# Whole loads of the moving operands at the changes of half, shared weight tiles and background key folds in a gated attention and MLP kernel

## The chip, the cores and the metric

The kernel runs on one core of a Trainium2 chip. The metric is the device time of one execution in microseconds. Five engines run side by side, each through its own queue in order: PE (TensorE) multiplies, and PEld is its loading of stationary tiles; DVE (VectorE) and ACT (ScalarE) do elementwise work; POOL (GpSimd) and SP (SyncE) here mostly issue DMAs. DMAs carry data between the large memory and the on-chip memory of 128 partitions.

## The reference

S = 2048 tokens, D = 1024, 32 heads of 32, DF = 3584. All in fp32.

```python
g = sigmoid((x * gate_w).sum(-1, keepdims=True))
a = A_ref(x, wqkv, w_phi, wo)
b = (gelu(x @ w_gate) * (x @ w_up)) @ w_down
return g * a + (1 - g) * b

def A_ref(x, wqkv, w_phi, wo):            # per head
    q, k, v = split(x @ wqkv)
    phi_q = concat([softmax(q @ w_phi), softmax(-(q @ w_phi))])
    phi_k = concat([softmax(k @ w_phi), softmax(-(k @ w_phi))])
    kv, z = phi_k.T @ v, phi_k.sum(tokens)
    o = (phi_q @ kv) / (phi_q @ z + 1e-6)
    return heads(o) @ wo
```

## The kernel before

**Split operands.** Every fp32 operand of a matmul is split into a high part in the short format fp32r, which ACT writes (`high`, L56), and a low part, the rest, which DVE subtracts (`low`, L59). A product is three passes, high·high, high·low and low·high (`PASSES`).

**Seven products for eight.** The large products of x are made on 2×2 blocks with seven block products in place of eight, from sums of blocks. The seven stationary operands of a unit come in four tiles: `wgu` for x (2 in turn), `tyz` for y and z (3 in turn), and `v`. The seven moving operands are the blocks x10, x11, x01 and the sums s1 to s4, each of four pieces of 128×512 (256 KB), split into high and low. `w_phi` is folded into the key and query weights by small matmuls (the folds: 16 key folds at L297, 16 query folds later), so that keys and queries come out already multiplied by it.

**Units and halves.** 80 units run one after another in `unit`. Half 0 has the eight value units `v`: the moving side is the value weights, the stationary side blocks of x. Half 1 has the eight key units `k`: the moving side is the folded key weights (`wk_fold`, and its sums `ks`), the stationary side again blocks of x. Half 2 and half 3 take one half of the tokens each as moving side (`in_xT` and its sums `xs`), with q, gate and up weights as stationary side: 4 query units and 14 pairs of gate and up. A unit has seven steps (slots) of one block product, 12 matmuls at L665: 0 a<-x, 1 p<-y, 2 c<-z of the unit before, 3 a<-z, 4 a<-v of the unit before, 5 c11<-x, 6 b<-y. Steps 0 and 3 start new sums in PSUM; ACT copies results on (`c<-b` L696, `c<-a` L709, `b<-a` L711), and DVE subtracts p from them (`less`, L678). Between steps stand fillers: query folds, features (L881) and attention (L1085).

**What sets the order.** A planner written in the kernel records everything in one order. `run_slot` takes, after each step, work from streams (generators that yield earliest slot, latest slot, DVE cost and ACT cost), as a clock of its own lets it fit; an engine's queue then holds its work in that order. SP's loads and POOL's stores are issued where the streams come to them.

**Turns.** Where the half changes (units 8, 16 and 48) all seven moving operands must be replaced while units go on. `change_half` has an order of parts with the step from which the old part is free and the step at which the new one is needed. There are three homes of 256 KB; a piece is loaded into a home (L480) once the piece that was there has been split by ACT and DVE.

**Weights.** `weights` makes the stationary operands of a unit: loads, sums on DVE (L133 to L141), splits. Units of half 2 store them, in part as sums (`tq..`, `tg..`), and half 3 loads them again (y and z: 1 MB each, L518).

**Start.** Unit 0 is done plainly while the value weights come in. Its raw pieces then give the sums s1 to s4 (`w_steps`, L146). Of the 16 key folds, 4 pieces at a time have homes; the others wait for a home and are put between the steps of units 1 and 2. `key_sums` then reads all of `wk_fold` back (4 MB), forms the sums and stores them as `ks`. `gates` forms g in the background.

**Values out.** `split_values` (L160 to L162) splits value results on ACT and DVE and stores them to `vt`, through three homes in turn.

**After the units** the down projection and `wo` run as one product at L1343, 3024 matmuls.

Of the kernel before, what the change touches and what calls it, by code (L numbers as in the profile page):

```python
# [16 lines left out]
P = 128  # L17
# [16 lines left out]
def tile_gated_mix(ctx: ExitStack, tc: tile.TileContext, x, xT, wkT, wqT, wv, w_phi, wo,  # L34
# [45 lines left out]
    def new_quarter(b, k):  # L80
        return ring.tile([P, 2, KC // 2, BLK], F32R, name=f"x{b % 2}{k}", bufs=1)
# [73 lines left out]
    def split_values(m, odd, j, i, dst, src):  # L155

        b, c, g = m // 4 * 2 + 1 - odd, m % 4, 4 * j + 2 * i
        d = dst.rearrange("p (n s d) -> p n s d", s=2, d=64)
        x = src[:, 256 * i:256 * i + 256].rearrange("p (n d) -> p n d", d=64)
        nc.scalar.activation(d[:, :, 0], x, AF.Copy)  # L160
        nc.vector.tensor_tensor(d[:, :, 1], x, d[:, :, 0].bitcast(F32), OP.subtract)
        nc.gpsimd.dma_start(tokens["v"][b][g:g + 2, :, c].rearrange("g p f -> p g f"),  # L162
                            dst.bitcast(F32).rearrange("p (g f) -> p g f", g=2))
# [16 lines left out]
    with tc.manual_schedule(engines={PE, DVE, ACT, SP}):  # L180
# [10 lines left out]
        xb, xs = {}, [None] * 4  # L191
# [26 lines left out]
        for b, k in ((1, 0), (1, 1), (0, 1)):  # L218
            xb[b, k] = new_quarter(b, k)
        x00 = [new_work(k, F32R).rearrange("p (a k) t -> p a k t", a=2) for k in range(2)]  # L220

        def x_plain(blk, kc):
            if (blk, kc // 4) == (0, 0):
                return x00[kc // 2][:, :, kc % 2]
            return xb[blk, kc // 4][:, :, kc % 4]
# [16 lines left out]
        def sum_steps(n):  # L242
            while n and ready:
                i = ready[0]
                if next(x_sums[i], "over") == "over":
                    ready.pop(0)
                    continue
                n -= 1

        bps = []  # L250
        for s in range(KC):
# [5 lines left out]
            high(xq[1][:, 0], src[1])  # L257
            if s == 0:
                nc.vector.tensor_copy(xq[0][:, 0], src[0])
            else:  # L260
                high(xq[0][:, 0], src[0])
            for blk in (1, 0):
                low(xq[blk][:, 1], src[blk], xq[blk][:, 0])
# [12 lines left out]
            for n, (a, e) in enumerate(PASSES):  # L276
                for blk in (1, 0):
                    for f in range(2):
                        nc.tensor.matmul(plain_banks[blk, f], wide_w[a][:, kc, f * P:(f + 1) * P], xq[blk][:, e],
                                         start=s == 0 and n == 0, stop=s == KC - 1 and n == 2)  # L280

        rooms = [stage().rearrange("p (a b) -> p a b", a=2)]
        first_o = stage((0, 1024, block("v", 3)))
        rooms.append(xa.tile([P, 2, BLK], F32, tag="v", name="fold", bufs=1))
        homes = [t[:, n] for t in rooms for n in range(2)]
        homes.append(fa.tile([P, BLK], F32, tag="o2", name="fold", bufs=1))
        order = [(h, kc) for h in range(2) for kc in range(KC)]

        def fold_load(i):
            h, kc = order[i]  # L290
            nc.sync.dma_start(homes[i], wkT[h, kc])

        def fold_piece(i):
            h, kc = order[i]
# [6 lines left out]
            if i in (2, 3, 4):  # L301
                fold_load(i + 3)
            elif 8 <= i < 12:
                fold_load(i + 4)

        for i in range(5):
            fold_load(i)
        split_0, raw_0 = new_work(0), new_work(1)
        homes += homes[2:] + [raw_0[:, n] for n in range(4)] * 2

        x1 = new_weight()
        y1 = xa.tile([P, 2, KC, P], F32R, tag="pts", name="first", bufs=1)
        xs = [(xa if k < 2 else fa).tile([P, 2, KC // 2, BLK], F32R, name=f"s{k + 1}", bufs=1) for k in range(4)]
        SUM_AT = (3, 0, 2, 1)

        def sum_parts(k, kc):
            src, dst = raws[kc][SUM_AT[k]], xs[k][:, :, kc]
            return (lambda: high(dst[:, 0], src)), (lambda: low(dst[:, 1], src, dst[:, 0]))
# [4 lines left out]
        def plain_store(n, j, f):  # L323
            for i in range(2):
                room = split_0[:, 2 * (n % 2) + i] if 2 * n + i < 7 else fp.tile([P, BLK], F32, tag="qx", name="vh", bufs=1)
                split_values(0, 1 - f, j, i, room.bitcast(F32R), raw_0[:, n])
# [19 lines left out]

        first_sums("y")
        sum_steps(100)
# [19 lines left out]
        def run_slot(t, matmuls=12, vector=0.0, scalar=0.0):  # L368
# [6 lines left out]
            while True:  # L375
                best = None
                for s in streams:
                    lo, hi, d, a = (*s[0], 0.0, 0.0)[:4]
                    d *= 0.91
# [38 lines left out]
        def key_sums(pa):  # L418
            for kc in range(KC // 2):
                rs = wide if kc % 2 else [pa[:, 0], pa[:, 1]]  # L420
                for r, j in zip(rs, (1, 0)):
                    nc.sync.dma_start(r.rearrange("p (a b) -> p a b", a=2), wk_fold[j][kc::4].rearrange("k p n -> p k n"))
                if kc % 2 == 0:
                    continue
                yield now[0] + 3, NEVER, 0.0
                for k in (kc - 1, kc):
                    r1, r2 = wide if k % 2 else [pa[:, 0], pa[:, 1]]
                    four = a11, a12, a21, a22 = r1[:, :BLK], r1[:, BLK:], r2[:, :BLK], r2[:, BLK:]
                    for i, _ in enumerate(w_steps(*four)):
                        if i % 2 == 0:  # L430
                            yield now[0], NEVER, 1.4
                    for i, t in enumerate((a22, a11, a21, a12)):
                        nc.gpsimd.dma_start(k_sum[i][:, k, :], t)
                yield now[0] + 1, NEVER, 0.0

        def gates(pa):
            rows = [pa[:, 1], wide[1]]
# [947 lines left out]
```

## Time and profile before

| | |
|---|---|
| median of 3 runs | 2459.62 us (2453.88 to 2465.41) |
| profiled execution | 2455.46 us |
| its span, first to last instruction | 2453.7 us |
| TensorE busy | 2367.0 us |
| mean granted TensorE clock | 0.980 |
| DMA | 657.49 MB, mean 268 GB/s |

Units start at 29.01 (unit 1), 74.24 (2), 97.81 (3), 209.79 (8, first turn), 279.97 (10), 407.07 (16, second turn), 463.73 (18), 1050.85 (47), 1073.57 (48, third turn), 1196.71 (53); the down projection follows from 1763.33. In a timeline row stand start, length (of a group: from its first start to its last end), engine, line, operation and tiles, and in brackets the idle time of that engine before it with what ended it. `x12` at the end counts the instructions in a group.

### The profile page before, as it was taken

The numbers are of one execution on the slowest core, as the hardware profiler recorded it, in microseconds if no ns is written. First come the engines' busy times: TensorE is split into PE (matmuls) and PEld (weight loads), VectorE is DVE, ScalarE is ACT, GpSimd is POOL, SyncE is SP. The second block draws the span as 40 slices with busy tenths as digits, with TensorE's granted clock in tenths as the row PEclk, the third lists the DMA queues.
The fourth block names the chain that finished last, engine by engine and source line by source line (L and its number), as shares of the span: only waits on it lengthen the run. The fifth ranks groups of instructions, "written<-read, shape, count | busy, mean of one in ns | idle before, by whom it ended". The sixth has DMA issues, their size and how long they took to land. (4 is left out here: it accounts for less than half of the span.)

```text
span 2453.7 us, 29604 instructions
## 1 busy us (share of the span) xinstructions
PE 2367.0 (96%) x10414; PEld 1939.4 (79%) x10414; DVE 1755.6 (72%) x2402; ACT 1212.1 (49%) x1702; POOL 393.7 (16%) x625
## 2 busy tenths in 40 slices
PE   7998999899999999988999999999999999999999
PEld 6875787678888888876788877878888888888887
DVE  7565556588887888754688888887375677876874
ACT  5434444555655565543578777776254223322221
POOL 2332332122222222211111111111000000000000
PEclk9998899999999999999999999999999999999999
DMA  6786787788888999989778877777686667887774
GB/s 210 269 297 229 258 280 282 266 297 304 306 294 301 304 296 311 313 308 328 235 258 248 261 253 238 252 234 255 228 307 234 222 232 251 303 296 281 266 276 137
DMA packets 244773, 657.49 MB, mean 268 GB/s; under 512 B 31360, under 2 KB 70288, under 8 KB 228240
## 3 DMA queue, kind: packets, MB, share of 16 engines
q1 hardware_dynamic: 184864, 436.53, 53.0%
q0 software_dynamic: 59488, 218.94, 25.7%
q8 instruction: 82, 1.34, 0.2%
q14 instruction: 67, 0.55, 0.1%
q10 hardware_dynamic: 272, 0.13, 0.0%
HBM read 436.86 MB, written 218.90 MB: 267 GB/s over the span
## 5 line engine op out<-in xcount | busy, mean ns | idle before, releaser
L1343 PE MATMUL po<-tw,wgu 128*128 128x512 f32 x1344 | 309.8, 389 | 0.0
L56 ACT ACTIVATE wgu<-stage 128x1024 fp32r<-128x1024 f32 (+2 forms) x168 | 174.6, 1039 | 250.1 <-DVE stage L1233 160.5
L1343 PEld LDWEIGHTS po<-tw,wgu 128*128 128x128 f32 x1344 | 252.3, 188 | 52.4
L665 PE MATMUL a<-s,tyz 128*128 128x512 f32 x948 | 243.1, 405 | 21.5 <-DMA tyz<-tq0z 5.9
L665 PE MATMUL c<-x,tyz 128*128 128x512 f32 x948 | 236.1, 398 | 18.0 <-ACT c L696 11.0
L665 PE MATMUL a<-x,wgu 128*128 128x512 f32 x948 | 234.9, 398 | 8.5 <-DVE wgu L59 6.7
L665 PE MATMUL b<-s,tyz 128*128 128x512 f32 x936 | 233.0, 398 | 9.2 <-ACT s L56 5.5
L665 PE MATMUL c<-x,wgu 128*128 128x512 f32 x948 | 235.1, 395 | 4.1 <-DVE x L59 2.4
L665 PEld LDWEIGHTS a<-s,tyz 128*128 128x128 f32 x948 | 182.8, 195 | 69.5 <-issue 14.9
L665 PE MATMUL p<-s,tyz 128*128 128x512 f32 x936 | 229.6, 394 | 5.4 <-ACT w L683 5.0
L665 PE MATMUL a<-s,v 128*128 128x512 f32 x948 | 230.8, 392 | 1.6 <-ACT s L56 1.1
L665 PEld LDWEIGHTS c<-x,tyz 128*128 128x128 f32 x948 | 180.7, 192 | 59.7 <-ACT c L696 13.1
L59 DVE TENSOR_TENSOR wgu<-stage,wgu 128x1024 fp32r<-128x1024 f32 (+2 forms) x136 | 162.9, 1197 | 88.5 <-ACT wgu L56 87.3
L665 PEld LDWEIGHTS a<-x,wgu 128*128 128x128 f32 x948 | 181.8, 193 | 48.0 <-DVE wgu L59 7.1
L665 PEld LDWEIGHTS b<-s,tyz 128*128 128x128 f32 x936 | 177.9, 191 | 51.7 <-ACT s L56 8.3
L665 PEld LDWEIGHTS p<-s,tyz 128*128 128x128 f32 x936 | 176.9, 190 | 45.8 <-ACT w L683 6.6
L665 PEld LDWEIGHTS c<-x,wgu 128*128 128x128 f32 x948 | 177.3, 190 | 44.1 <-DVE x L59 4.6
L665 PEld LDWEIGHTS a<-s,v 128*128 128x128 f32 x948 | 178.4, 189 | 40.6 <-ACT s L56 2.0
L1343 PE MATMUL po<-tw,wl 128*128 128x512 f32 x672 | 156.9, 389 | 0.0
L1343 PE MATMUL po<-tyz,wgu 128*128 128x512 f32 x672 | 155.6, 389 | 0.4 <-DVE wgu L59 0.4
L1343 PEld LDWEIGHTS po<-tyz,wgu 128*128 128x128 f32 x672 | 126.0, 188 | 27.0 <-DVE wgu L59 0.8
L1343 PEld LDWEIGHTS po<-tw,wl 128*128 128x128 f32 x672 | 126.0, 188 | 26.3 <-DVE wl L59 0.2
(331 smaller groups left out, 3600.3 us busy)
## 6 DMA issues: line engine op xcount, KB each, us to landing
stage<-lm SPq DMA_DIRECT2D x98, 512.0 KB, 4.5
sr<-in_w_down SPq DMA_DIRECT2D x84, 512.0 KB, 4.9
sl<-lm SPq DMA_DIRECT2D x70, 512.0 KB, 4.8
lm<-h POOLq DMA_DIRECT2D x112, 256.0 KB, 5.7
stage<-in_w_gate SPq DMA_DIRECT2D x42, 512.0 KB, 6.4
stage<-in_w_up SPq DMA_DIRECT2D x42, 512.0 KB, 5.2
vs<-vt SPq DMA_DIRECT2D x32, 512.0 KB, 4.3
zs<-w POOLq DMA_DIRECT2D x32, 512.0 KB, 6.3
```

The lines of the kernel that those rows point to most:

```text
L56: nc.scalar.activation(dst, src, AF.Copy)
L59: nc.vector.tensor_tensor(dst, src, dst_h.bitcast(F32), OP.subtract)
L665: nc.tensor.matmul(dst, w[:, h, 4 * part + kc, :], xq[:, e, kc, :], start=first and kc == 0 and i == 0, stop=kc == 3 and i == 2, skip_grou ...
L1343: nc.tensor.matmul(ps[c], lefts[s][:, a, m, c * P:(c + 1) * P], made[k][:, e, m], start=d == 0 and m == 0 and n == 0, stop=d == n_duo - 1 ...
```

## The change

1. **Moving operands as whole halves.** Each of the seven operands now has a tile for its high and one for its low parts (`x_part`). `change_half` loads all four pieces of an operand at one point (L509), into a home that a table `PLANS` names: the rings of `wgu` ("x") or `tyz` ("y"), the work tiles, or the low tile of another operand that isn't written yet (a number). `change_parts` and `low_part` split them.
2. **Shared weights.** `shares(n)`: units 7 and 8 (value and key block 7) and units 47 and 48 (query block 3 in both halves) use the same stationary tiles. The order of the key units and of the queries in half 3 is changed to that end; the sums of that query block are neither stored nor loaded.
3. **Key folds.** Four folds stand before unit 1; the other twelve are fillers in units 2 to 5 (`key_folds`), with their sums formed from the tiles at hand. Only one group of four pieces is read back. `gates` starts after the first turn.
4. **Copy and subtraction.** At step 0, `move` puts ACT's copy c<-b ahead of DVE's subtraction in halves 0 to 2 (`swap`).
5. **Values out.** Both halves are split together, over four homes.
6. **y and z in half 3** are loaded in two parts of 512 KB (L596).
7. **Start.** The first weight's split and the folds stand ahead of the sums; in unit 1 the steps 1 and 5 are exchanged.
8. The planner counts 0.95 of a DVE cost in place of 0.91. The accumulators of the down projection get other names; its work is the same.

**First place: DVE before unit 1.** The row `wgu<-stage,wgu` of 128×1024 is the low half of the first weight, `raw` and `h` at L146 (now L149) the sums s1 to s4, `first` is y. Before:

```order
L59 TENSOR_TENSOR first_546<-stage_534,first_546 128x1024 [waits Activation_49]
L146 TENSOR_TENSOR raw_342<-raw_342 128x512
L146 TENSOR_TENSOR raw_342<-raw_342 128x512 [waits DVE_49]
L146 TENSOR_TENSOR raw_343<-raw_343 128x512
L146 TENSOR_TENSOR raw_343<-raw_343 128x512 [waits DVE_49] x3
L146 TENSOR_TENSOR raw_347<-h_346,raw_347 128x512
L146 TENSOR_TENSOR h_346<-h_346,h_344 128x512 [waits DVE_49]
L146 TENSOR_TENSOR h_344<-h_344,raw_347 128x512 [waits DVE_49]
L146 TENSOR_TENSOR h_345<-h_345,h_344 128x512 [waits DVE_49]
L59 TENSOR_TENSOR wgu_545<-stage_381,wgu_545 128x1024 [waits Activation_49]
```

Now:

```order
L59 TENSOR_TENSOR wgu_546<-stage_384,wgu_546 128x1024 [waits DMAHW1_49,Activation_49]
L136 TENSOR_TENSOR stage_537<-stage_537 128x512 [waits DMAHW2_49]
L137 TENSOR_TENSOR stage_537<-stage_384,stage_537 128x512 [waits DVE_49]
L59 TENSOR_TENSOR first_547<-stage_537,first_547 128x1024 [waits Activation_49]
L149 TENSOR_TENSOR raw_347<-h_346,raw_347 128x512
L59 TENSOR_TENSOR s1l_549<-raw_341,s1h_548 128x512 [waits Activation_49]
L59 TENSOR_TENSOR s1l_549<-raw_342,s1h_548 128x512 [waits Activation_49]
L59 TENSOR_TENSOR s1l_549<-raw_343,s1h_548 128x512 [waits Activation_49]
L59 TENSOR_TENSOR s1l_549<-raw_347,s1h_548 128x512 [waits Activation_49]
L149 TENSOR_TENSOR raw_342<-raw_342 128x512
L149 TENSOR_TENSOR raw_343<-raw_343 128x512
L149 TENSOR_TENSOR h_346<-h_346,h_344 128x512
```

The first weight's low half has moved from behind ten sums to ahead of them; the remaining sums are spread between later low halves.

**Second place: SP at the third turn**, around unit 48. L480 and L509 are pieces of moving operands, L64 and L534 (L612) a unit's raw and x weights, L518 (L596) y and z. Before:

```order
L480 DMA w0_543<-xs00_152 128x512 x2
L587 DMA o2_8037<-wq7_190 128x512
L480 DMA w0_543<-xs01_153 128x512 x4
L64 DMA stage_8083<-wq2_185 128x1024
L534 DMA wgu_8085<-tq1x_309 128x1024
L480 DMA w0_543<-in_xT 128x512
L518 DMA tyz_8108<-tq0z_307 128x2048
L480 DMA w0_543<-in_xT 128x512 x3
L600 DMA o2_8150<-wq1_184 128x512
L480 DMA w0_543<-xs02_154 128x512 x2
```

Now:

```order
L509 DMA wx_7946<-in_xT 128x512 x4
L509 DMA wy_7970<-xs00_152 128x512 x4
L509 DMA wx_7946<-xs01_153 128x512 x4
L509 DMA s2l_8041<-in_xT 128x512 x4
L669 DMA o2_8046<-wq7_190 128x512
L918 DMA vs_2849<-vt1_149 128x1024
L509 DMA wy_7970<-xs02_154 128x512 x4
L64 DMA stage_8109<-wq0_183 128x1024
L612 DMA wgu_8111<-tq0x_305 128x1024
L509 DMA w0_544<-in_xT 128x512 x3
```

The pieces of an operand, which stood singly among other loads, stand four together, into tiles of several names in place of w0 alone.

**Third place: ACT and DVE at step 0 of a unit in half 2**, here the one in whose turn h_5759 is written. `c_87<-b_86` is the copy, `h_5759<-b_86,w0` the subtraction; the names after "waits" are the semaphores of the engine or DMA queue. ACT before:

```order
L683 ACTIVATE w0_543<-p_5604 128x512 [waits DVE_49]
L56 ACTIVATE v_5752<-o2_5703 128x512 [waits DMAHW6_49,DMASW6_49]
L696 ACTIVATE c_87<-b_86 128x512 [waits DVE_49]
L56 ACTIVATE tyz_5778<-stage_5598 128x1024 [waits DMASW5_49,PE_49]
L858 ACT_TABLE_LOAD
```

ACT now:

```order
L769 ACTIVATE w0_544<-p_5603 128x512 [waits DVE_49]
L56 ACTIVATE v_5749<-o2_5702 128x512 [waits DMAHW7_49,DMASW3_49]
L783 ACTIVATE c_87<-b_86 128x512 [waits PE_49,Activation_49]
L56 ACTIVATE tyz_5777<-stage_5598 128x1024 [waits DMASW2_49]
L948 ACT_TABLE_LOAD [waits DMASW5_49]
```

DVE before:

```order
L678 TENSOR_TENSOR h_5759<-b_86,w0_543 128x512 [waits DMASW4_49,PE_49,Activation_49]
L634 TENSOR_TENSOR h_5759<-h_5759,w0_543 128x512 [waits DVE_49]
L59 TENSOR_TENSOR v_5752<-o2_5703,v_5752 128x512 [waits DMAHW6_49,DMASW6_49,Activation_49]
L59 TENSOR_TENSOR tyz_5778<-stage_5598,tyz_5778 128x1024 [waits DMASW5_49,Activation_49]
L861 TENSOR_REDUCE st_5782<-w1_565 128x32 [waits Activation_49]
```

DVE now:

```order
L764 TENSOR_TENSOR h_5759<-b_86,w0_544 128x512 [waits DMASW1_49,Activation_49]
L716 TENSOR_TENSOR h_5759<-h_5759,w0_544 128x512 [waits DVE_49]
L59 TENSOR_TENSOR v_5749<-o2_5702,v_5749 128x512 [waits DMAHW7_49,DMASW3_49]
L59 TENSOR_TENSOR tyz_5777<-stage_5598,tyz_5777 128x1024 [waits DMASW2_49,PE_49,Activation_49]
L951 TENSOR_REDUCE st_5781<-w1_599 128x32 [waits Activation_49]
```

The places in the queues are the same; only the direction of the wait has turned: ACT waited for DVE, and now DVE waits for ACT.

The core of the diff:

```diff
+    X_NAMES = ("x10", "s1", "s2", "x11", "s3", "s4", "x01")
+    def x_part(i, part, dtype=F32R):
+        pool = ring if i % 3 == 0 else xa if i < 3 else fa
+        return pool.tile([P, KC // 2, BLK], dtype, name=X_NAMES[i] + "hl"[part], bufs=1)
...
         def change_half(t, half):
...
-            homes = [gated(1, 0), *((e2[:, 0], e2[:, 1]) if half == 1 else (gated(0, 0), gated(0, 1)))]
...
+            homes = {}
+            for i, at, home in PLANS[half]:
+                yield t + at, t + at, 0.0
+                while home in busy:
+                    yield now[0] + 1, now[0] + 1, 0.0
...
+                busy[home] = True
+                for j in range(len(x)):
+                    nc.sync.dma_start(x[j], srcs[i][:, j])
+                start(change_parts(half, i, home, x, t, need, srcs[i]))
+        LAST, NEED, busy = (-7, -6, -4, -2, -1, 4, 2), (0, 1, 3, 5, 6, 11, 9), {}
+        SPARE = ((0, -7, "x"), (1, -6, "y"), (2, -4, "x"), (3, -3, 2), (4, -1, "y"))
+        PLANS = {1: (*SPARE, (6, 0, "x"), (5, 3, "y")), 3: (*SPARE, (6, 0, "g"), (5, 3, "z")),
+                 2: ((0, -11, "x"), (2, -5, 1), (1, -5, "x"), (3, -1, "x"), (4, 0, 3), (5, 3, 6), (6, 4, "x"))}
...
+        def shares(n):
+            return n in TURNS and units[n][2] == units[n - 1][2] and units[n][1] + units[n - 1][1] in ("kv", "qq")
...
-                load_parts("z", z)
+                load_part("z", z, 0)
+                yield t + 1, t + 1, 0.0
+                load_part("z", z, 1)
...
-        def move(c, b):
-            subs.append(subs.pop()())
+        def move(c, b, swap=False):
+            if not swap:
+                subs.append(subs.pop()())
             nc.scalar.activation(c, b, AF.Copy)
+            if swap:
+                subs.append(subs.pop()())
...
-                    move(c, b)
+                    move(c, b, before[0] < 3)
...
+            if n and shares(n):
+                right_ops[n] = right_ops[n - 1]
...
+        def key_folds(i, groups):
...
+            for kc in groups:
+                for (h, c), t in zip(pieces, four):
+                    nc.sync.dma_start(t, wkT[h, c] if kc else wk_fold[h][c])
...
+                    fillers.append((0, products, 4, range(1, 7)))
```

In a plan a row is the operand's number, the step from the turn at which its load is issued, and its home.

More of the change, by code (lines that the diff above doesn't have):

```diff
@@ L497, in tile_gated_mix, with low_part @@
+        def low_part(dst, x, h, need, home, j):
+            yield now[0], need - 2, 0.69
+            low(dst, x, h)
+            if j == KC // 2 - 1:
+                del busy[home]
+                if home == "z":
+                    for k in held_homes:
+                        held[k] = False
         HALF = {2: 1, 3: 0}
-        units = [(0, "v", m) for m in range(8)] + [(1, "k", m) for m in (4, 5, 6, 7, 0, 1, 2, 3)]
+        units = [(0, "v", m) for m in range(8)] + [(1, "k", m) for m in (7, 4, 5, 6, 0, 1, 2, 3)]
@@ L511, in weights @@
             seen.add((kind, m))
+            if n + 1 < len(units) and shares(n + 1):
+                again = {}
+            chunk = kind == "k" or kind == "v" and shares(n + 1)
             def keep_parts(i, t):
@@ L557, in weights @@
                     mine["y"] = y
[L558 removed]
+                    if chunk:
                         store_chunk(m, 2, 0, o)
```

295 lines of the change are left out of this document (167 added, 128 removed).

## The prediction

> **What bounds the kernel now.** I read the page's busy table first, then the table of stretches, cut where the kernel turns from one half to the next.
>
> ```profile
> span 2453.7 us, 29604 instructions
> PE 2367.0 (96%) x10414; PEld 1939.4 (79%) x10414; DVE 1755.6 (72%) x2402; ACT 1212.1 (49%) x1702; POOL 393.7 (16%) x625
> 27.31:97.81 70.50, 54.30 (x273) 46.12 (x272) 41.09 (x65) 36.32 (x70) 21.20 (x33) 0.88 0.61 207
> 97.81:209.79 111.98, 102.81 (x421) 80.59 (x419) 72.34 (x118) 43.81 (x81) 37.21 (x55) 0.95 0.81 277
> 209.79:279.97 70.18, 58.32 (x192) 40.17 (x193) 36.34 (x56) 30.17 (x54) 17.25 (x24) 0.81 0.70 230
> 407.07:463.73 56.66, 46.54 (x170) 32.37 (x168) 28.36 (x40) 25.22 (x39) 7.71 (x13) 0.94 0.77 277
> 463.73:1050.85 587.12, 584.11 (x2669) 485.57 (x2668) 476.43 (x624) 340.12 (x451) 143.87 (x235) 1.00 0.89 301
> 1050.85:1196.71 145.86, 126.17 (x525) 101.08 (x524) 70.71 (x105) 55.95 (x92) 24.35 (x41) 0.94 0.86 303
> ```
>
> The columns are the stretch, its length, the busy time of PE, PEld, DVE, ACT and POOL, then granted clock, DMA share and GB/s. TensorE is busy for 96% of the span, and the change takes no matmul away: what can be won is what TensorE waits, and the clock that it loses around its waits. The stretches are the start (units 1 and 2), the value units 3 to 7, turn 1 (units 8, 9), turn 2 (16, 17), the body of half 2 (18 to 46) and turn 3 (47 to 52).
>
> Next comes the price of an undisturbed step, from the timeline of TensorE (start, length, group):
>
> ```profile
> 91.47 1.05 PE L297 MATMUL misc<-bp,w 128*128 128x128 f32 x8
> 92.28 2.98 PE L665 MATMUL c<-x,wgu 128*128 128x512 f32 x12
> 397.94 1.11 PE L881 MATMUL misc<-pts,vs 128*128 128x256 f32 x8
> 398.89 2.91 PE L665 MATMUL a<-s,v 128*128 128x512 f32 x12
> 1146.66 2.88 PE L665 MATMUL c<-x,wgu 128*128 128x512 f32 x12
> 1149.38 2.88 PE L665 MATMUL b<-s,tyz 128*128 128x512 f32 x12
> ```
>
> From start to start a product step (12 matmuls) costs 2.72 us, a fold 0.81, a feature filler 0.95. A unit has 7 steps, so the loss of a stretch is its length less these:
> - start: 70.50 − 12 steps (32.64) − 16 folds (12.96) = **24.9**
> - values: 111.98 − 35 steps (95.2) = **16.8**
> - turn 1: 70.18 − 14 steps (38.08) − 3 fillers (2.4) = **29.7**
> - turn 2: 56.66 − 14 steps (38.08) = **18.6**
> - half 2: 587.12 − 203 steps (552.2) − 232 filler matmuls (29 groups of 8 at 0.95, 27.6) = **7.3**
> - turn 3: 145.86 − 42 steps (114.24) − 3 fillers (2.8) = **28.8**
>
> Together 126 us. TensorE's waits proper are length less busy (11.9 in turn 1, 10.1 in turn 2, 19.7 in turn 3); the rest is slow clock (0.81 granted in turn 1).
>
> ```profile
> 1069.12 4.61 PE L665 MATMUL b<-s,tyz 128*128 128x512 f32 x12 [1.79 <-ACT b L711]
> 1141.12 2.98 PE L665 MATMUL a<-s,tyz 128*128 128x512 f32 x12 [1.50 <-DMA tyz<-tq2z]
> ```
>
> The bracket is the idle time before. After 1.79 us the next step took 4.61 instead of 2.88, after 1.50 only 2.98: a wait of about 1.8 us or more costs 1.7 us again in slow clock. The Trainium skill, "TensorE: Matmul & The Clock Gate", section "HAM oscillation — how this bites in real kernels", puts the limit at "no PE-idle gaps >~3.4µs"; this trace pays at 1.79 already, and the measurement decides. By that rule removing turn 1's short gaps would give back the gaps alone; that is a rival below.
>
> **The change part by part.**
>
> *Start, 24.9.*
>
> ```profile
> 28.23 4.20 DVE L146 TENSOR_TENSOR raw<-raw 128x512 f32<-128x512 f32 x6
> 35.13 1.22 DVE L59 TENSOR_TENSOR wgu<-stage,wgu 128x1024 fp32r<-128x1024 f32 x1
> 36.40 3.90 PE L665 MATMUL a<-x,wgu 128*128 128x512 f32 x10 [6.68 <-DVE wgu L59]
> 50.12 2.05 PE L297 MATMUL misc<-bp,fold 128*128 128x128 f32 x8 [4.38 <-DMA fold<-in_wkT]
> ```
>
> The first weight's low half stood behind the sums on DVE; it now stands ahead of them, so the 6.68 goes, and its slow step. Folds that waited for reloads (4.38 here) become fillers taken when their data are there; their 16 × 0.81 us on TensorE stay. But the sums (each 0.70, six in the row of 4.20) now stand ahead of later operands: step 3 of unit 1 waits for z behind six of them and two of its own sums (8 × 0.70 = 5.6), and step 1 of unit 2 for a low half that stands behind a value store. I keep 20 of the 24.9: **−5**. Bounds: +5, if both waits come at full length with a slow step, to −13 (both gaps above with 1.7 each, no new wait).
>
> *Values, 16.8.*
>
> ```profile
> 189.39 4.77 PE L665 MATMUL p<-s,tyz 128*128 128x512 f32 x12 [2.30 <-ACT w L683]
> 215.71 0.38 ACT L160 ACTIVATE w<-c 128x256 fp32r<-128x256 f32 x1 [4.38 <-DMA vt<-w]
> ```
>
> ACT's split waits for the store that last used its home, and the copy of p stands behind it: such a stall costs TensorE 2.30 + 1.89. A fourth home gives each store one more split of time; ACT's wait is still there at times, but shorter than what TensorE has in hand. Against this twelve folds with their loads (3 MB) and sums run here. I keep about two stalls of 4.2: **−8**, bounds −13 (one) and +4 (five, if fold fillers wait for their data).
>
> *Turns 1 and 2, 29.7 and 18.6.*
>
> ```profile
> 228.91 0.63 ACT L56 ACTIVATE s<-w 128x512 fp32r<-128x512 f32 x1 [3.26 <-DMA w<-ks]
> 233.30 0.63 ACT L56 ACTIVATE x<-w 128x512 fp32r<-128x512 f32 x1 [3.77 <-DMA w<-wk]
> 421.84 0.63 ACT L56 ACTIVATE x<-w 128x512 fp32r<-128x512 f32 x1 [3.72 <-DMA w<-in_xT]
> 2100.00:2160.00 60.00, 60.00 (x266) 49.71 (x265) 50.30 (x50) 18.35 (x18) 3.79 (x7) 1.00 0.94 340
> ```
>
> Each of 28 pieces is loaded only when one of three homes has been converted: the latency of a 256 KB load stands in the chain again and again, with DMA only 0.70 busy. The new plan asks for four pieces at once, most parts two to five steps (5 to 14 us) ahead of need, so a latency is paid once a part and mostly beside matmuls. Converting a part is 4 × 0.63 on ACT and 4 × 0.69 on DVE, about 2.8 us, one step. Turn 1 also loses unit 8's weights, 1.25 MB of loads and their splits. What is left is the rate: turn 1 moved 70.18 × 230 = 16.1 MB, less 1.25 is 14.9; at 340 GB/s, the rate in the last row, 43.8 us against 40.5 without loss. Turn 2's 56.66 × 277 = 15.7 MB take 46.2 against 38.1, part of it loaded earlier. I leave 6.7 in each, about 1.6 stalls of 4.2: **−23** and **−12**. Bounds: one half of the loss kept (−15, −9), or two thirds of a stall left (−27, −16).
>
> *Turn 3, 28.8.*
>
> ```profile
> 1077.76 0.42 SPq L518 DMA_DIRECT2D tyz<-tq0z x1
> tyz<-tq0z SPq DMA_DIRECT2D x1, 1024.0 KB, 9.9
> 1087.81 5.46 PE L665 MATMUL a<-s,tyz 128*128 128x512 f32 x12 [5.88 <-DMA tyz<-tq0z]
> 1117.56 4.74 PE L665 MATMUL a<-s,tyz 128*128 128x512 f32 x12 [2.82 <-DMA tyz<-tq1z]
> stage<-in_w_gate SPq DMA_DIRECT2D x42, 512.0 KB, 6.4
> ```
>
> The z operand, 1 MB, is asked for at the unit's start and needed 3 steps (8.2 us) later, and takes 9.9. Unit 48 now shares unit 47's weights: 3.5 MB of loads and 2.75 MB of stores go, and with them the 5.88 and its slow step (2.58). The later z loads come in halves; step 3 needs the first alone, and 512 KB takes 6.4 by the last row, so 2.82, 1.50 and two more of its kind shrink to little. Part loads go ahead as in turn 2. The stretch moved 145.86 × 303 = 44.2 MB; 38 MB take 112 us at 340 GB/s, under the 117 without loss. I leave two stalls, 8.8: **−20**; bounds −10 (the parts' 1 MB loads take the place of z) and −26.
>
> *Half 2 and the swap, 7.3.*
>
> ```profile
> 708.87 0.69 DVE L678 TENSOR_TENSOR w<-b,w 128x512 f32<-128x512 f32 x1 [1.96 <-PE b L665]
> 712.40 0.58 ACT L696 ACTIVATE c<-b 128x512 f32<-128x512 f32 x1
> 712.53 1.22 DVE L861 TENSOR_REDUCE st<-w 128x32 f32<-128x1024 f32 x1 [1.77 <-ACT w L858]
> 715.91 1.23 DVE L59 TENSOR_TENSOR tyz<-stage,tyz 128x1024 fp32r<-128x1024 f32 x1 [1.77 <-ACT tyz L56]
> 716.76 2.99 PE L665 MATMUL a<-s,tyz 128*128 128x512 f32 x12
> ```
>
> ACT's copy of b now goes first and DVE's subtraction waits for it: a wait is added on DVE. Behind it stand the low half of v, the reduction and the low half of z, which TensorE takes at 716.76. If the copy still ends at 712.98, then 0.69 + 0.69 + 1.22 + about 0.35 bring DVE to 715.93 for the z half, which began at 715.91: no loss, but no cover either. The copy itself can go earlier, since it no longer waits for DVE. **−1** for the half with the k units; bounds −4 and +10 (a third of 29 units late by 1 us).
>
> *Half 3.*
>
> ```profile
> 1224.81 0.69 DVE L678 TENSOR_TENSOR h<-b,w 128x512 f32<-128x512 f32 x1 [3.71 <-DMA la<-h]
> 1226.17 4.61 PE L665 MATMUL c<-x,tyz 128*128 128x512 f32 x12 [3.48 <-ACT c L696]
> ```
>
> DVE waits for the spill of an h buffer, ACT's copy for DVE, TensorE for both: 3.48 + 1.73. The swap is not made in this half, so the mechanism stays; the new order has the tight place five times instead of six. **−2**, bounds 0 and −5. The down projection's work is as before.
>
> **Sum:** −5 −8 −23 −12 −20 −1 −2 = −71. The profiled execution took 2455.46 us, 1.8 more than its span; 2455.46 − 71 = **2384**. It lies 4.2 under the median of the three runs shown, which spread over 11.5, so I add nothing. The bounds add up to −95 and −15 when each term ends at the same side, which they seldom do.
>
> **Rivals.**
> - *The waits move.* Whole parts of 1 MB arrive as late as pieces did, since the same bytes (less 7.5 MB) go through queues that are 0.86 busy in turn 3, and new waits in the start and the folds come in full. Half of the turns' gain is kept (28), the start and values give 5: 2455 − 36 = 2419. For it: DMA share 0.81 to 0.89 outside turn 1. Against: turn 1's 0.70 and 230 GB/s say latency, not rate. Chance 0.22.
> - *The slow clock stays.* If short gaps are not what slows the clock, only the gaps go: turn 1 then gives 11.9 less a 3 left, 9, not 23; turn 2 about 7, not 12: 2403. Against: every slow step listed follows a wait. Chance 0.06. (That is what the Trainium skill's page on TensorE, cited above, would give.)
> - *All clean.* Terms near their good ends, −95 to −105: about 2352. Chance 0.12.
> - *Little happens.* The loads ahead find their homes still in use, since each plan reuses halves and rings that units read until late; the turns keep all but the shared weights (−8 for the 5.88 and its slow step): 2448. Chance 0.05.
> - *Slower through the swap.* If ACT's copy comes over 0.2 us later than at 712.98, every unit of half 2 has its z half late; from a slip of about 1 us a gate of 1.8 us is reached in the worse steps and 1.7 of slow clock joins: 29 × 2.7 = 78, so 2384 + 78 = 2462. For it: there is no cover at 715.91. Against: ACT is 58% busy in half 2 (340.12 of 587.12), and the copy is not placed later. Chance 0.08.
>
> The forecast itself has 0.47. Forecast, clean, clock and moved waits hold 0.87; the range runs from the clean case to beyond the moved waits, 2350 to 2434. A measurement of this kernel tells 0.5% (12 us) from no change: faster 0.85, same 0.07, slower 0.08.
>
> **What would show it.** Turn stretches at a granted clock over 0.95; no piece-by-piece waits of ACT for part loads; no wait of step 3 of unit 48; z waits under 1 us; the first product at about 31 us, and unit 3 by about 93; DVE's z half in half 2 no later than 7.4 us after a unit's start. It is wrong if ACT waits over 4 us for whole parts, if fold fillers hold TensorE in units 4 and 5, or if half 2 grows by over 10 us.

## The result and the profile after

The changed kernel took **2370.22 us** (median of 3 runs, 2370.14 to 2370.99) against 2459.62 before (2453.88 to 2465.41): a ratio of 0.9637, 95% interval 0.9601 to 0.9674. Its profiled execution took 2370.22, 85.2 less than the 2455.46 of before; the forecast was 71 less, 2384.

The table by stretches of the changed kernel, cut at the same units as before (stretch, length, busy time of PE, PEld, DVE, ACT and POOL, granted clock, DMA share, GB/s):

```profile
27.40:84.98 57.58, 44.48 (x193) 34.98 (x192) 40.70 (x66) 31.31 (x59) 14.95 (x22) 0.88 0.57 187
84.98:189.77 104.79, 104.55 (x502) 87.84 (x500) 65.61 (x107) 48.97 (x96) 44.48 (x68) 1.00 0.79 274
189.77:230.50 40.73, 40.73 (x194) 34.04 (x192) 31.75 (x50) 25.97 (x48) 16.45 (x23) 1.00 1.02 361
358.01:407.75 49.74, 42.54 (x178) 33.83 (x177) 35.08 (x48) 27.14 (x44) 10.12 (x18) 0.93 0.86 317
407.75:989.49 581.74, 580.90 (x2671) 484.88 (x2669) 475.09 (x624) 337.18 (x448) 142.43 (x233) 1.00 0.88 303
989.49:1127.91 138.42, 124.83 (x525) 102.02 (x524) 79.27 (x122) 59.47 (x100) 24.10 (x40) 0.94 0.80 275
1127.91:1679.03 551.12, 549.25 (x2418) 453.18 (x2417) 443.11 (x740) 401.92 (x587) 73.80 (x116) 1.00 0.81 255
```

The last row, from unit 53 to the down projection, has this one of the kernel before to stand beside, with as many matmuls:

```profile
1196.71:1763.33 566.62, 555.48 (x2418) 457.14 (x2417) 452.58 (x758) 399.53 (x591) 75.43 (x118) 0.99 0.76 246
```

Turn 1 is the plainest: TensorE is busy for all of its 40.73 us, at full clock. Turns 2 and 3 still stand at a clock of 0.93 and 0.94. Less steps and fillers, as in the prediction (6 of the 16 folds are now in the start, 10 in the value units; one feature filler has moved from the key units into turn 2), the losses are:

| stretch | loss before | loss after | gain | forecast |
|---|---|---|---|---|
| start | 24.9 | 20.1 | 4.8 | 5 |
| values | 16.8 | 1.5 | 15.3 | 8 |
| turn 1 | 29.7 | 0.2 | 29.5 | 23 |
| turn 2 | 18.6 | 10.7 | 7.9 | 12 |
| half 2, with the key units | | | 4.0 | 1 |
| turn 3 | 28.8 | 21.4 | 7.4 | 20 |
| half 3 from unit 53 | | | 15.5 | 2 |

The sum was near by luck, because errors of both signs met: turn 3 gave 13 too little, half 3 13 too much. What TensorE's products still wait for, the longest waits of its timeline:

```profile
43.69 0.80 PE L751 MATMUL a<-s2h,tyz 128*128 128x512 f32 x1 [4.98 <-ACT tyz L56]
64.94 1.22 PE L751 MATMUL p<-s1h,tyz 128*128 128x512 f32 x2 [5.08 <-DVE tyz L59]
378.22 0.79 PE L751 MATMUL c<-x11h,wgu 128*128 128x512 f32 x1 [4.29 <-ACT x11h L56]
1040.98 0.79 PE L751 MATMUL p<-s1h,tyz 128*128 128x512 f32 x1 [5.25 <-ACT w L769]
1071.86 0.47 PE L751 MATMUL a<-s2h,tyz 128*128 128x512 f32 x1 [2.96 <-DMA tyz<-tq1z]
1095.37 0.47 PE L751 MATMUL a<-s2h,tyz 128*128 128x512 f32 x1 [2.61 <-DMA tyz<-tq2z]
```

A feature filler in unit 47 also waits 2.76 us, at 1008.73; the view names no releaser for it. Behind the third and fourth row stand these rows of ACT and SP:

```profile
362.26 2.38 SPq L509 DMA_DIRECT2D x11l<-xs  x4
369.86 0.63 ACT L56 ACTIVATE s3h<-x11l 128x512 fp32r<-128x512 f32 x1 [7.33 <-DMA x11l<-xs]
377.55 2.18 ACT L56 ACTIVATE x11h<-w 128x512 fp32r<-128x512 f32 x4
1027.28 0.34 SPq L553 DMA_DIRECT2D w<-in_xT  x1
1037.26 0.63 ACT L56 ACTIVATE x01h<-w 128x512 fp32r<-128x512 f32 x1 [7.91 <-DMA w<-in_xT]
1040.35 0.58 ACT L769 ACTIVATE w<-p 128x512 f32<-128x512 f32 x1
```

At turn 2 the pieces of s3, asked for 4 us into the turn, land 7.6 to 15 us after that. They lie in the tile that x11's low part will take, and the splits of x11, for which TensorE waits, stand behind theirs in ACT's queue. At turn 3 the fourth piece of x01 has no home of its own: it is asked for when the first has been split (1027.28), lands ten us later, and the copy of p stands behind its split.

The two waits for z at the end have different beginnings. Units 50 and 51 start at 1060.6 and 1084.4; L596 is z; `kz` is attention's first load of the key features' closing sums, which waits for the stores of these sums:

```profile
1062.61 0.53 SPq L596 DMA_DIRECT2D tyz<-tq1z  x1
1082.91 7.85 SPq L1062 DMA_DIRECT2D kz<-kz  x2
1090.86 1.18 SPq L596 DMA_DIRECT2D tyz<-tq2z  x2
```

In unit 50 the first half is asked for 2 us after the unit's start and TensorE gets on 9.3 us later; in unit 51 it is asked for only 6.5 us after the start, since SP stood at the kz loads for 7.85, and TensorE gets on 4.5 us after that.

### The profile page after: what moved, and what is told of

It is laid out like the page before. It is cut to its first block, busy times and chain, and to the rows that moved or that the text cites. A ratio compares the mean times of both kernels' runs of the same rounds, so it can differ in the third digit from the quotient of the medians.

```text
span 2368.4 us, 29632 instructions
## 1 busy us (share of the span) xinstructions
PE 2325.5 (98%) x10414; PEld 1925.8 (81%) x10414; DVE 1744.5 (74%) x2394; ACT 1210.1 (51%) x1702; POOL 388.7 (16%) x618
## 5 line engine op out<-in xcount | busy, mean ns | idle before, releaser
L751 PE MATMUL a<-s2h,tyz 128*128 128x512 f32 x632 | 212.5, 397 | 12.9 <-ACT tyz L56 5.0
L751 PE MATMUL p<-s1h,tyz 128*128 128x512 f32 x624 | 208.6, 396 | 14.0 <-DVE tyz L59 7.8
L751 PE MATMUL c<-x11h,wgu 128*128 128x512 f32 x632 | 209.7, 393 | 6.0 <-ACT x11h L56 4.3
L751 PE MATMUL c<-x01h,tyz 128*128 128x512 f32 x632 | 208.2, 390 | 0.2 <-ACT c L783 0.2
L751 PE MATMUL a<-s4h,v 128*128 128x512 f32 x632 | 208.4, 391 | 0.0
L751 PE MATMUL a<-x10h,wgu 128*128 128x512 f32 x632 | 207.9, 390 | 0.3 <-DVE wgu L59 0.3
L751 PE MATMUL b<-s3h,tyz 128*128 128x512 f32 x624 | 205.7, 390 | 0.0
L751 PEld LDWEIGHTS a<-s2h,tyz 128*128 128x128 f32 x632 | 120.4, 191 | 41.1 <-ACT tyz L56 5.4
L751 PEld LDWEIGHTS c<-x11h,wgu 128*128 128x128 f32 x632 | 119.8, 190 | 31.4 <-ACT x11h L56 4.7
L751 PEld LDWEIGHTS a<-s4h,v 128*128 128x128 f32 x632 | 119.1, 189 | 24.8
```

The lines of the kernel that those rows point to most:

```text
L751: nc.tensor.matmul(dst, w[:, h, 4 * part + kc, :], xq[e][:, kc, :], start=first and kc == 0 and i == 0, stop=kc == 3 and i == 2, skip_grou ...
```

## The experiments

Twelve kernels, each timed beside the kernel before; stretches are from their profiles, one for each kernel. Stretches that an edit doesn't touch differ by some us too: turn 3 is 2.6 longer in experiments 1 and 10 than in the changed kernel, turn 2 in experiment 7 is 4.8 longer than before. The changed kernel was not timed again beside the later ones.

**1. Without the turned wait** (the copy c<-b behind DVE's subtraction again):

```diff
-                    move(c, b, before[0] < 3)
+                    move(c, b)
```

> The changed kernel, but with DVE's subtraction ahead of ACT's copy c<-b again in every half. Theory A, the turned wait is what brought half 2 from 587.1 to 581.7 us: half 2 goes back by 4 to 6 and the time is 2374 to 2377. Theory B, half 2 lost only one wait of a filler and its slow steps, which the turned wait has nothing to do with: half 2 stays within 1 of 581.7, the time is 2369 to 2372. In neither does half 3 (551.1) change, since the change turned no wait there.

Measured: 2368.66 (2368.17, 2369.15), half 2 at 580.61, 1.1 shorter. Theory B, a little past its bounds of 1 us and 2369. The turned wait brings nothing, and costs 1 us at most.

**2. The planner's factor alone undone:**

```diff
-                    d *= 0.95
+                    d *= 0.91
```

> The changed kernel with the planner's factor for DVE costs back at 0.91. Theory A, the factor moved the attention output's copy and spill ahead of a unit's start in half 3, and so took away the three stalls of 3.4 to 3.9 us there: they come back, half 3 grows from 551.1 to 560 to 567, the time is 2380 to 2387. Theory B, the place of the spills came from the other parts, which shifted the background work against the units: half 3 stays within 3, the time is 2368 to 2374.

Measured: 2398.51 (2398.36, 2398.66). Neither theory had the place: half 3 stays, half 2 grows by 34.8, turn 3 shrinks by 10.1. The stretch of half 2 in the table by stretches:

```profile
412.75:1029.27 616.52, 594.96 (x2694) 488.44 (x2693) 519.31 (x697) 350.96 (x473) 153.98 (x250) 0.99 0.88 297
```

And DVE and TensorE in its timeline, at one of its feature fillers:

```profile
591.59 1.22 DVE L59 TENSOR_TENSOR pts<-w,pts 128x1024 fp32r<-128x1024 f32 x1
592.90 1.55 PE L971 MATMUL misc<-pts,vs 128*128 128x256 f32 x8 [2.30 <-issue]
```

The filler stands in TensorE's queue ahead of its operand: DVE ends the low half of pts at 592.81, the filler starts at 592.90, after a wait that the view puts down to nothing. Waits of 0.5 to 2.3 us, 13.6 in all, stand before ten such fillers in this half. With 0.91 the planner counts less time for DVE and put them too early; with 0.95 no such wait stands there. That is a part of the 34.8: DVE also has 697 instructions in the stretch in place of 624, so work from later has moved into it, and the rest was not taken apart.

**3. The factor alone in the kernel before:**

```diff
-                    d *= 0.91
+                    d *= 0.95
```

> The kernel before, with nothing but the planner's factor for DVE costs at 0.95. Theory A, the higher factor keeps feature fillers from standing ahead of their operands, in any kernel of this form: half 2 falls from 587.1 by 2 to 6, nothing else moves by over 3: 2449 to 2456. Theory B, 0.91 costs 35 us in half 2 only with the other parts of the change, which make DVE fuller there, and 0.95 means more waiting elsewhere: within 3 of before or slower.

Measured: ratio to before 1.0005, 0.999 to 1.0021 (2459.59, 10 runs). Half 2 falls to 580.58, 6.5 less, and its wait of 2.36 us on pts is gone: Theory A there, a little past its 6. But turn 3 grows to 149.55, and the part from unit 53 to the end to 1264.85 from 1257.0, with five stalls on c<-b. The time is within 3 of before, as in Theory B. By itself the factor gives nothing; with the other parts its lack costs 28 us.

**4. Weights not shared:**

```diff
-            return n in TURNS and units[n][2] == units[n - 1][2] and units[n][1] + units[n - 1][1] in ("kv", "qq")
+            return False and n in TURNS and units[n][2] == units[n - 1][2] and units[n][1] + units[n - 1][1] in ("kv", "qq")
```

> The changed kernel, but units 8 and 48 make or load their own weights again. Theory A, sharing is a good part of the turns' gain: turn 1 (40.7) grows by 3 to 8, and in turn 3 (138.4) the wait for unit 48's z with its slow step is back, 8.5; the time is 2382 to 2388. Theory B, the loads ahead alone do it and the shared weights only save traffic that fits anyway: both turns within 3, the time within 2367 to 2375.

The values of this kernel differ from those of the changed one, and why is not known; the matmuls are as many. Its turns 1 and 3 by stretches:

```profile
191.92:238.80 46.88, 43.24 (x194) 35.04 (x192) 32.75 (x51) 26.62 (x47) 17.02 (x24) 0.96 0.99 336
998.91:1151.63 152.72, 123.57 (x526) 99.47 (x524) 74.57 (x111) 58.60 (x98) 24.86 (x42) 0.93 0.85 290
```

In the timelines of SP and TensorE stand, in units 47 and 48:

```profile
1015.47 1.76 SPq L509 DMA_DIRECT2D wx<-in_xT  x4
1025.35 0.79 PE L751 MATMUL b<-s3h,tyz 128*128 128x512 f32 x1 [9.96 <-ACT b L800]
1051.62 0.76 PE L751 MATMUL a<-s2h,tyz 128*128 128x512 f32 x1 [7.72 <-DMA tyz<-tq3z]
```

Measured: 2393.50 (2393.05, 2393.96). Turn 1 grows by 6.2, turn 3 by 14.3, and the wait for unit 48's z is back at 7.72. Theory A in its mechanism, but 5.5 over its range. The longest wait is another: unit 48's own x weight now takes a tile of the wgu ring, so the pieces of x10 are asked for 16.6 us after the start of unit 47, when step 5 of that unit has read the other tile; in the changed kernel they are asked for 2.5 us ahead of that start. ACT stands at their split, with the copy b<-a behind it, and TensorE waits 9.96. The plan of the loads counts on the shared weights, so the 14.3 is not the price of z alone.

**5. Moving operands piece by piece again**, by the loop of the kernel before with its three homes in place of the plan:

```diff
-            for i, at, home in PLANS[half]:
+            order = ((0, -7, 0), (1, -6, 1), (2, -4, 3), (3, -2, 5), (4, -1, 6), (6, 2, 9), (5, 4, 11))
+            parts = [(i, j, t + free + 1, t + need) for i, free, need in order for j in range(KC // 2)]
+            homes = [gated(1, 0), *((e2[:, 0], e2[:, 1]) if half == 1 else (gated(0, 0), gated(0, 1)))]
...
+                if n + 3 < len(parts):
+                    load(n + 3)
```

> The changed kernel, but the moving operands are loaded piece by piece through three homes again, at the steps of the kernel before; shared weights, background folds and all else stay. Theory A, the whole loads ahead make the turns' gain: turn 1 goes from 40.7 to 55 to 65, turn 2 from 49.7 to 55 to 57, and turn 3 by 5 or more; the time is 2395 to 2410. Theory B, freeing ACT, DVE and queues of other work at the turns (shared weights, no gate products, no read back) makes it: turn 1 stays under 48, the time under 2382.

At the first turn the homes meet the value stores, which now use gated(1,0) too: value halves overwrite pieces that wait there, so values of half 1 are others, with as many matmuls. Its turns 1 and 2 by stretches:

```profile
189.35:249.53 60.18, 49.15 (x193) 36.15 (x192) 30.15 (x47) 27.50 (x51) 15.67 (x22) 0.91 0.77 254
379.81:444.98 65.17, 52.05 (x170) 35.34 (x168) 28.89 (x40) 26.40 (x41) 7.92 (x14) 0.84 0.72 250
```

Measured: 2424.51 (2422.93, 2426.09). Turn 1 is 19.5 longer, turn 2 15.4; turn 3 is 1.7 shorter. Theory A for turn 1; turn 2 goes beyond its 57, and turn 3 does not follow. At 65.17 turn 2 is also 8.5 longer than in the kernel before with the same loop, so its 15.4 is more than what the whole loads win there. From unit 53 on another 19.4 are lost, in part in waits of the last attention fillers (3.06 and 1.41 us), for the rest not explained.

**6. y and z loaded whole again in the changed kernel**, and **7. in halves in the kernel before:**

```diff
-                    load_part("y", y, 0)
-                    yield max(now[0], t - 2), t - 2, 0.0
-                    load_part("y", y, 1)
+                    load_parts("y", y)
...
-                load_part("z", z, 0)
-                yield t + 1, t + 1, 0.0
-                load_part("z", z, 1)
+                load_parts("z", z)
```

(experiment 7 is the same with the signs turned.)

> The changed kernel, but y and z in half 3 are loaded whole again (1 MB each, y at four steps ahead, z at its unit's start). Theory A, the 1 MB loads at a unit's start are what delayed the spills of h in half 3 and so made the three stalls of 3.4 to 3.9 us: stalls of TensorE on the copy c<-b come back, the part from unit 53 on grows from 1240.5 by 8 to 16; turn 3 grows too, as z needs 1 MB by step 3: the time is 2382 to 2392. Theory B, the spills moved against the units through another part: from unit 53 on within 3 of 1240.5, and only turn 3 grows, by 2 to 8: 2371 to 2379.

> The kernel before, with nothing but the loads of y and z in half 3 made in two halves, as in the changed kernel. Theory A, these halves alone let the spills of h land in time: the three stalls from unit 53 on (3.48, 3.43, 3.88) go or shrink below 1, that part falls from 1257.0 us by 8 to 15, and the z waits of turn 3 shrink by 3 to 8: 2435 to 2448. Theory B, it also takes the other place of the attention work against the units: the stalls stay within 1 us, only turn 3 gains: 2448 to 2456.

Measured for the first: 2387.45, from two runs far apart (2376.39, in Theory B's range, and 2398.51, beyond Theory A's); the profiled one, the slower, is 21.7 longer from unit 53 on (1262.19 against 1240.49) and 4.4 in turn 3. In it three stalls on c<-b are back (2.99, 5.62, 3.80); one of them, in the timelines of SP, POOL, DVE and TensorE:

```profile
1284.04 0.32 SPq L595 DMA_DIRECT2D tyz<-tg4z  x1
1284.65 0.56 POOL L133 DMA_DIRECT2D la<-h  x1 [7.64 <-ACT h L1164]
1293.70 0.69 DVE L763 TENSOR_TENSOR h<-b,w 128x512 f32<-128x512 f32 x1 [7.51 <-DMA la<-h]
1295.07 0.80 PE L750 MATMUL c<-x01h,tyz 128*128 128x512 f32 x1 [5.62 <-ACT c L782]
```

The 1 MB load and the spill are asked for within 0.6 us, and the spill lands nine us later. As the faster run has no profile, the second experiment carries more. For the second: ratio 0.9975, 0.9961 to 0.9988 (2453.27, 10 runs); from unit 53 on 1249.28, 7.7 less, though turn 3 is 6.2 longer where Theory A had it shrink. The time lies in Theory B's range. One place, unit 74, which starts at 1633.32 before and at 1634.74 with halves, has its spill issued within 0.1 us of that start in both. Timelines of POOL, DVE and TensorE, before:

```profile
1633.34 0.56 POOL L130 DMA_DIRECT2D la<-h  x1 [4.21 <-ACT h L1075]
1641.44 0.69 DVE L678 TENSOR_TENSOR h<-b,w 128x512 f32<-128x512 f32 x1 [4.65 <-DMA la<-h]
1642.81 4.62 PE L665 MATMUL c<-x,tyz 128*128 128x512 f32 x12 [3.88 <-ACT c L696]
```

With halves:

```profile
1634.74 0.56 POOL L130 DMA_DIRECT2D la<-h  x1 [8.20 <-ACT h L1083]
1639.85 0.69 DVE L686 TENSOR_TENSOR h<-b,w 128x512 f32<-128x512 f32 x1 [1.65 <-DMA la<-h]
1641.21 3.01 PE L673 MATMUL c<-x,tyz 128*128 128x512 f32 x12 [0.87 <-ACT c L704]
```

The other two stalls of before, 3.48 and 3.43, with halves:

```profile
1229.20 3.02 PE L673 MATMUL c<-x,tyz 128*128 128x512 f32 x12 [1.24 <-ACT c L704]
1476.14 3.02 PE L673 MATMUL c<-x,tyz 128*128 128x512 f32 x12 [0.59 <-ACT c L704]
```

Beside the whole loads DVE could go on 8.1 us after the spill's issue, beside halves 5.1. Theory A in its mechanism for the spills: with nothing but the halves the three stalls shrink from 10.8 us to 2.7, which covers the 7.7, half of the 15.5. In the changed kernel the spill is also issued 1.6 us ahead of such a unit's start (1592.07 against 1593.65, unit 76), which the halves alone don't bring; what moved it was not taken apart.

**8. The closing sums of the key features held back:**

```diff
-                elif not fjobs and finishing[0] == 1:
+                elif not fjobs and finishing[0] == 1 and now[0] >= 7 * 50 + 6:
```

> The changed kernel, with the closing sums of the key features (zs and kz loads) held back until step 6 of unit 50. Theory A, these loads (4 MB and small ones on which SP stands) fall among the z loads of units 50 and 51 and make the waits of 2.96 and 2.61 us there: the waits shrink below 1 and turn 3 falls from 138.4 by 4 to 9, if attention, which starts later, doesn't run late at the end: 2361 to 2366. Theory B, the z loads are late by their own size at that DMA load: waits stay over 2, turn 3 within 2, the time 2369 to 2373.

TensorE's timeline:

```profile
1115.23 0.77 PE L751 MATMUL a<-s2h,tyz 128*128 128x512 f32 x1 [3.60 <-DMA tyz<-tg0z]
1140.11 0.77 PE L751 MATMUL a<-s2h,tyz 128*128 128x512 f32 x1 [4.14 <-DMA tyz<-tu0z]
```

Measured: 2377.42 (2376.52, 2378.32), slower. The waits for the z of units 50 and 51 are gone and turn 3 is 3.6 shorter, but waits for z now stand at units 52 and 53, where the loads of the closing sums went, and from unit 53 on 8.4 are lost. Theory A in its cause (z is late because of these loads), wrong in its price: the waits moved with them.

**9. x01 a step earlier at turn 3**, **10. s3 ahead of x11 at turn 2**, **11. both and the value stores of unit 2 later**, **12. both alone** (9 changes the row of turn 3 in the plan, 10 that of turn 2, 12 both, 11 also the last line):

```diff
-        PLANS = {1: (*SPARE, (6, 0, "x"), (5, 3, "y")), 3: (*SPARE, (6, 0, "g"), (5, 3, "z")),
-                 2: ((0, -11, "x"), (2, -5, 1), (1, -5, "x"), (3, -1, "x"), (4, 0, 3), (5, 3, 6), (6, 4, "x"))}
+        PLANS = {1: (*SPARE, (6, 0, "x"), (5, 3, "y")), 3: (*SPARE[:4], (6, -1, "g"), SPARE[4], (5, 3, "z")),
+                 2: ((0, -11, "x"), (2, -5, 1), (1, -5, "x"), (4, -1, 3), (3, -1, "x"), (5, 3, 6), (6, 4, "x"))}
...
-            2: {0: puts[:2], 1: [lambda: sum_steps(100), lambda: split_sums(3, kcs=(2, 3))], 2: puts[2:]}}
+            2: {1: [*puts[:2], lambda: sum_steps(100), lambda: split_sums(3, kcs=(2, 3))], 2: puts[2:]}}
```

> The changed kernel, with the load of x01 at turn 3 issued one step earlier and ahead of s3's. Theory A, its fourth piece, which is loaded only when the first has been split (ACT waited 7.91 us for it with the copy of p behind), makes TensorE's 5.25 us wait in unit 49: with the first pieces there sooner the wait falls below 2, turn 3 by 4 to 7, and the time to 2363 to 2367. Theory B, the transfers in the stretch are bound by rate, and the wait moves to s3 or z: within 2 of 2370.

> The changed kernel, with s3 loaded ahead of x11 at turn 2. Theory A, s3 lands late because its load stands last, and ACT waits for it (7.33 us) with the splits of x11 behind: TensorE's wait of 4.29 us goes and turn 2 falls from 49.7 by 4 to 7, to 2363 to 2367. Theory B, DMA is bound by rate there (317 GB/s over the stretch): x11 lands as late as s3 did, and the time stays within 2 of 2370.

> The changed kernel with three edits: s3 ahead of x11 at turn 2, x01 one step earlier at turn 3, and the first value stores of unit 2 issued one step later, behind the low half of y for which TensorE waited 5.08 us. Theory A, the three waits have nothing to do with each other: gains of 5, 4.5 and 5 to 7 add up, 2354 to 2357. Theory B, the stores' wait is met anyway by the next work on DVE: the start gains under 2, the time is 2359 to 2363.

> The changed kernel with two edits, s3 ahead of x11 at turn 2 and x01 one step earlier at turn 3; the value stores of unit 2 stand as in the changed kernel. Theory A, moving those stores cost the start 2.4 us (60.0 against 57.6) by two new waits, and the two turn edits add up to what each gave alone (5.1 and 4.5): 2359 to 2362, the start at 57.2 to 58.2. Theory B, the start's 2.4 is scatter between runs, and the turn edits share one gain: 2362 to 2366.

The stretch of turn 3 with x01 earlier, TensorE's wait in unit 49 there, and the stretch of turn 2 with s3 first:

```profile
990.14:1125.00 134.86, 122.98 (x525) 100.42 (x524) 79.73 (x122) 59.74 (x100) 24.13 (x40) 0.96 0.84 282
```

```profile
1038.53 0.50 PE L751 MATMUL p<-s1h,tyz 128*128 128x512 f32 x1 [3.15 <-ACT w L769]
```

```profile
357.14:402.16 45.02, 40.54 (x178) 32.20 (x176) 34.55 (x48) 25.76 (x42) 10.00 (x17) 1.00 0.98 355
```

Measured: 2365.70 (2364.41, 2366.99), wait 5.25 to 3.15, not below 2, and turn 3 3.6 shorter: in its time Theory A, in its stretch a little under it; and 2365.13 (2364.10, 2366.16), turn 2 4.7 shorter at full clock, Theory A. All three edits: 2362.68 (2361.19 to 2368.50), in Theory B's range, but the start grew to 60.00 from 57.58. TensorE's timeline in unit 2 there:

```profile
60.61 1.20 PE L751 MATMUL p<-s1h,tyz 128*128 128x512 f32 x2 [1.61 <-DVE tyz L59]
69.81 0.50 PE L751 MATMUL a<-s2h,tyz 128*128 128x512 f32 x1 [2.31 <-ACT tyz L56]
72.72 1.22 PE L751 MATMUL a<-s2h,tyz 128*128 128x512 f32 x2 [2.18 <-DVE tyz L59]
```

The 5.08 shrinks to 1.61, and two waits for the next operand take its place. Without that edit the start is 58.08 again, as Theory A had it, and the time 2364.17 (2358.54 to 2365.74, 5 runs), in Theory B's range. Turn 2 gives 3.3 and turn 3 4.2 in this profile, 7.5 of the 9.6 that the two edits were expected to add up to. The two best versions can't be told apart. Both medians lie 6 to 8 us below the changed kernel's, but by the ratio to the kernel before, timed beside each, the gain is not shown: 0.9612 (0.959 to 0.9633) and 0.9621 (0.9602 to 0.964) against 0.9637 (0.9601 to 0.9674), and 0.9638 and 0.9636 for experiments 9 and 10. What shows it is the stretches: turn 2 is 45.0 to 46.8 in the three kernels with s3 first and 49.4 to 50.1 in experiments 1, 4, 6, 8 and 9; turn 3 is 134.2 to 134.9 in the three with x01 earlier, and 138.4 to 141.1 in the changed kernel and experiments 1 and 10.

## Why the prediction was right, and where it was not

- **Bound and sum: right.** Only TensorE's waits and slow clock were there to win; the down projection and the matmuls stayed. −85 came against −71, inside the range. Two slips stand in the working: the good bounds of the terms add up to −104, not −95, and the DMA share outside turn 1 was 0.61 to 0.89 by the rows shown (start 0.61, turn 2 0.77), not 0.81 to 0.89. The measured −85 lies inside both sums.
- **Slow clock goes with the waits: right**, for the rival "the slow clock stays" fell: turn 1 had 11.9 us of waits and gave 29.5. The limit that I read from two rows, about 1.8 us, doesn't hold, though. A row of the kernel before that I passed over:

```profile
1162.82 2.96 PE L665 MATMUL a<-s,tyz 128*128 128x512 f32 x12 [2.40 <-DMA tyz<-tq3z]
```

  After 2.40 us the step took 2.96, as if undisturbed, where 1.79 had cost 4.61. Length alone doesn't decide it. The Trainium skill, "TensorE: Matmul & The Clock Gate", section "What's actually happening", says of the window in which activity is judged that it is "free-running". The granted clock of this trace agrees. In turn 3 it fell to 0.50 in just three stretches:

```profile
1070.10:1073.50 3.40, 3.40 (x9) 2.65 (x9) 1.81 (x3) 1.26 (x2) 0.36 (x1) 0.50 0.87 316
1087.20:1094.00 6.80, 6.19 (x15) 4.86 (x16) 2.77 (x4) 4.31 (x7) 0.54 (x1) 0.50 0.64 212
1114.50:1121.30 6.80, 3.98 (x10) 3.00 (x10) 3.81 (x5) 3.83 (x7) 0.00 (x0) 0.50 0.80 308
```

  They are 3.4, 6.8 and 6.8 us long, and they start 17.1 and 27.3 us after one another, 5 and 8 times 3.41: the clock changed on a grid. Where a wait falls on that grid may be what spared the 2.40; no run tried it.
- **Start: right** (20.1 left, 20 forecast), with both new waits as named, 4.98 and 5.08, and the waits of before (6.68 on the first weight, 4.38 on a fold) gone.
- **Values and turn 1: the mechanism right, the term too small.** I left 8.8 and 6.7 for stalls of 4.2 that did not come: 1.5 and 0.2 were left. The 340 GB/s that I took as a limit for turn 1 was exceeded, 361 there at a DMA share of 1.02. Experiments 4 and 5 give sharing 6.2 and whole loads 19.5 of turn 1. For the values no experiment parts the fourth home from the rest.
- **Turn 2: too large by 4.** The step "a latency is paid once a part and mostly beside matmuls" failed for s3, whose load the plan places behind that of x11, and ACT's queue passed its lateness to x11. Experiment 10 shows it.
- **Turn 3: too large by 13.** The step "The later z loads come in halves", by which the waits "shrink to little", failed: two waits of 2.96 and 2.61 stayed, since loads of the closing sums of the key features fall among them (experiment 8). In unit 50 TensorE could go on 9.3 us after the first half was asked for, where I had taken 6.4, and in unit 51 it was asked for 6.5 us late, behind a kz load on SP. And "part loads go ahead as in turn 2" did not hold for the fourth piece of x01 (experiment 9). The 8.5 that I gave to sharing fits the wait of 7.72 and its slow step in experiment 4; the 14.3 there hold also the wait for the ring tile, which I had not seen as a price of the plan.
- **Half 3: missed.** "The mechanism stays" was right, "the tight place five times instead of six" was the wrong step: what I counted were places in the order, and what decides is when the spill lands. I costed the halves of y and z where they are waited for and not for what else is in the queues beside them.
- **Half 2: the sign right by luck.** The swap did nothing (experiment 1), so my 0.02 us of slip was a fair reading and the rival on the slow side did not happen. But the 5.4 us that half 2 won are not the copy's: I gave the planner's factor no line at all, and alone in the kernel before it takes 6.5 from that half (experiment 3). With the other parts in place it is worth 28 us.
- **Signs: mixed.** One sign of being wrong came: ACT waited over 4 us for whole parts, 7.33 and 7.91. Of the signs of being right, two stayed away: turns 2 and 3 stood under a clock of 0.95, and z waits were over 1 us. As said came the first product, at 30.95, no wait in step 3 of unit 48, and units 4 and 5 without waits for folds.

## What to carry to other kernels

A number in a planner is a part of the change like any other: price it by the fillers that stand ahead of their operands. When a large load is split or moved, ask which small store is issued at the same moment and who waits for it. And where a plan loads operands whole, look at the part whose load stands behind the others and at the one piece without a home of its own; their lateness is passed on through the queue of the engine that splits them.

## What was not expected of the hardware

At the same place in unit 74 the reader of the 256 KB spill went on 5.1 us after its issue beside two loads of 512 KB, and 8.1 beside one of 1 MB. In turn 1 the core moved 361 GB/s over 40.7 us, above the 340 of the row that I had taken for a limit; a row of the kernel before as long as that shows more still:

```profile
2129.00:2169.73 40.73, 40.73 (x181) 33.74 (x180) 37.56 (x39) 13.77 (x14) 2.17 (x4) 1.00 1.00 378
```
